# A planned attention kernel: the shared SBUF port in the planner's clock, head groups evened, the opening loads and the last unit's normalisation rearranged

## The chip, the core and the metric

The kernel runs on one core of a Trainium2 chip. Five engines each run their own queue of instructions in order and meet only at semaphores: TensorE (PE, with its weight loads shown as PEld), ScalarE (ACT), VectorE (DVE), GpSimd (POOL) and SyncE (SP), which here only starts DMA transfers. ACT starts a few transfers too. The metric is device time in microseconds of the whole program. The kernel before took 675.31 us (median of 7 runs, 674.93 to 677.05).

## The reference, cut to what matters

Two attention blocks over 2048 tokens of width 512, with 32 heads of 16 columns each; their outputs stand side by side.

```python
qkv = (x @ wqkv)  # -> q, k, v per head, 32 heads of 16
# A: linear attention
phi = lambda t: jnp.where(t > 0, t + 1, jnp.exp(t)) + 1e-6
o = (phi(q) @ (phi(k).T @ v)) / (phi(q) @ phi(k).sum(0) + 1e-6)
# B: full softmax attention
p = softmax(q @ k.T * 16 ** -0.5)
o = p @ v
# both: o, heads joined, @ wo; A in columns 0:512, B in 512:1024
```

Block B is nearly all of the work: 32 heads of 2048 x 2048 exponentials.

## The kernel before, in words

**Units and blocks.** B is cut into 32 units, taken in order. A unit is a group of eight heads (`Gp`, four of them), a chunk of 512 queries (`c`, four), and the even or odd heads of the group (`e_`, two): four heads, one for each of the four 32-row bands of TensorE ("head group" g). Each of these four heads has 16 blocks of 128 keys x 512 queries, so a unit has 64 blocks and the kernel 2048.

**What a block goes through.** A score matmul on PE (L785, 32 rows; blocks of different g run side by side in different bands) puts 128x512 scores into a PSUM bank. Then one of two engines makes the exponential. ACT takes two or three banks in one instruction (L1000), each block leaves one tile, and one matmul with the values (L1129, "PV", into a 32-column band of the bank `PVb`; again four g side by side) uses it. Or DVE takes one bank, sometimes two (L886): it makes an exponential of low precision by integer arithmetic on the bits, POOL makes two shifted copies (L1075, `int64_add`, mostly two blocks an instruction), and the three copies are weighted and averaged by three PV matmuls with weights folded into copies of V (L632). So a block on DVE spares ACT its share, and costs PE three PV matmuls in place of one, DVE one instruction and POOL two halves.

**Closing a unit.** When all PV matmuls of a unit are done, `unit_done` (L1149) has DVE transpose `PVb` (L1153), take the reciprocal of the sums (L1160), multiply (L1161) and, after every second unit, transpose back into the output operand `ON` (L1167). The next unit's PV matmuls can start after L1153. The last unit's four output tiles (`last_tiles`, L1190) have three quarters of their matmuls done ahead; the fourth (L1181) waits for L1167, then DVE and ACT copy two tiles each (L526), and each tile is stored by a DMA (L1201), from SP's queue for DVE's tiles and from ACT's for ACT's.

**The planner.** The order of all instructions is fixed when the program is built, by a simulated clock: `T` holds the time at which each engine comes free, `cands` the ready stages with a planned length, `opts` the next choice of each engine, and the earliest goes next. `fill_act_cand` gives blocks to ACT (two or three from `choose`), with blocks for DVE (`d_pick`) put into the same score phase up to four in all; `fill_d_cand` gives DVE more; `pv_cand` forms PV batches of one or two, sometimes three, rounds of up to four g; `job_cand` fits in the projections and block A; `fill_in` puts dummy matmuls (L1351) into gaps of PE. `d_pick` gives DVE a block only if DVE's planned backlog is small. `choose` takes the head groups by "not used in this phase", then most blocks left. `TABLE` holds eleven settings of these rules for each 20 us of planned time (waits, backlogs, batch sizes, reserves). The planner knows nothing of DVE and POOL holding each other up. The chip runs the queues in the planned order, whenever the semaphores let it.

**The opening.** ACT's queue loads tokens 256 to 511 of B_x (L384, into `ON[:, 2:4]`) and the K weights of group 0; SP's queue loads tokens 0 to 255 with a transposing DMA (L393), the Q weights of group 0, tokens 512 to 1023 (transposing), the V weights, and the rest. PE runs 30 warm-up matmuls (L1209), transposes the two plain tiles (L1220; copies by DVE and ACT, L526), and projects the first K and Q tiles (L1231), which DVE and ACT copy out (L1239, L1241, L1243). The planner's clock starts behind this with written-in times.

Of the kernel before, what the change touches and what calls it, by code (L numbers as in the profile page):

```python
# [17 lines left out]
class _Op:  # L18
    __slots__ = ("idx", "lane", "fn", "pos", "waits", "sig", "count", "vc",
                 "name", "queue")  # L20

# [219 lines left out]
def bass_concat_heads__linear_attn_block__softmax_full_mha__prompt_kernel(nc, A_x, A_wqkv, A_wo, B_x, B_wqkv, B_wo, out):  # L241
# [34 lines left out]
        (3, 0.1, 1.0, 0, 16, 8, 2, 0.8, 0, 4.0, 4),  # L276
        (3, 0, 1.0, 0.6, 16, 8, 2, 0.8, 0, 4.0, 4),
        (1, 0.05, 2.0, 1.0, 16, 11, 2, 0.8, 0.5, 3.0, 6),
        (1, 0.05, 2.0, 0.6, 16, 11, 2, 2, 0.5, 3.0, 8),
        (1, 0.05, 2.0, 1.0, 8, 12.5, 2, 2, 0.5, 3.0, 8),  # L280
        (2, 0.3, 0.6, 0, 5, 8, 3, 0.8, -0.5, 4.0, 4),
        (2, 0.3, 0.6, 0, 5, 13.5, 2, 0.8, -0.5, 4.0, 4),
        (3, 0.3, 0.6, 0, 16, 13.5, 2, 0.8, -0.5, 4.0, 4),
        (3, 0.3, 0.6, 0, 16, 13.5, 2, 0.8, 0.8, 4.0, 8),
        (3, 0.05, 0.6, 1.0, 6, 9, 2, 0.8, 0.5, 4.0, 4),
        (3, 0.05, 1.0, 0.6, 16, 13.5, 3, 0.8, 0.2, 3.0, 4),
        (2, 0.2, 0.3, 0.6, 12, 8, 2, 0.8, 0.5, 2.0, 4),
        (1, 0.2, 1.5, 0.6, 3, 11, 2, 0.8, 0.5, 4.0, 6),
        (1, 0.2, 1.5, 0.3, 3, 11, 2, 0.8, 0.5, 4.0, 6),
        (2, 0.2, 1.5, 0.3, 3, 12.5, 2, 0.8, 0.2, 2.0, 8),  # L290
        (2, 0.2, 1.5, 0, 3, 9, 2, 0.8, 0.2, 2.0, 8),
        (3, 0.05, 0.6, 0.6, 12, 8, 2, 0.8, 0.2, 2.0, 6),
        (3, 0.2, 0.6, 0.6, 12, 10, 2, 2, -0.5, 3.0, 8),
        (3, 0.1, 1.0, 0.3, 8, 10, 2, 2, 0.2, 4.0, 8),
        (1, 0.2, 1.5, 0.3, 8, 9, 2, 0.8, 0, 4.0, 8),
        (2, 0.3, 1.0, 1.0, 16, 9, 2, 2, 0.2, 3.0, 6),
        (2, 0, 0.3, 1.0, 16, 9, 2, 2, 0.2, 3.0, 6),
        (2, 0.2, 1.5, 0, 12, 13.5, 3, 0.8, 0.2, 4.0, 8),
        (3, 0.3, 2.0, 0, 12, 12.5, 2, 0.8, 0, 2.0, 8),
        (1, 0, 2.0, 1.0, 5, 13.5, 2, 0.8, 0, 3.0, 8),  # L300
        (1, 0.3, 2.0, 0, 12, 13.5, 2, 0.8, 0.5, 3.0, 8),
        (2, 0.05, 2.0, 0, 12, 11, 2, 0.8, 0.5, 3.0, 8),
        (2, 0.05, 2.0, 0, 12, 11, 2, 0.8, 0.2, 3.0, 8),
        (3, 0.3, 1.0, 1.0, 3, 10, 2, 2, -0.5, 4.0, 6),
        (2, 0, 2.0, 1.0, 16, 11, 2, 0.8, 0, 4.0, 8),
        (1, 0.2, 2.0, 0.6, 16, 10, 2, 2, 0.8, 2.0, 4),
        (1, 0, 1.5, 0.3, 16, 8, 2, 0.8, -0.5, 3.0, 8),
        (1, 0, 2.0, 1.0, 5, 12.5, 2, 0.8, 0.8, 4.0, 6),
# [10 lines left out]
    with es:  # L319
# [75 lines left out]
        load(ON[:, 2:4, :], B_x[0].rearrange("(t p) c -> p t c", p=128)[:, 2:4, :], on_keys(2) + on_keys(3), queue="act")  # L395
        load_t(xTb, "xTb", B_x, 0, 2)
        load(Wb[:, :, 512:640], wbv[:, :, 512:640], [("Wb", 1, 0)], queue="act")
        load(Wb[:, :, 0:128], wbv[:, :, 0:128], [("Wb", 0, 0)])
# [220 lines left out]
        def v4_job(t4, Gp, **kw):  # L619
# [11 lines left out]
            for k in (1, 2):  # L631
                st.append(("dve", 0.2, f_op("dve", lambda e, k=k: e.tensor_scalar(  # L632
                    VV[:, r, k, 4 * t4:4 * t4 + 4, :], VV[:, r, 0, 4 * t4:4 * t4 + 4, :], WGT[k], None, op0=ALU.mult),
                    [("VV", t, r) for t in ts] + [("VV1", r)], [("VW", k, t, r) for t in ts])))
# [6 lines left out]
        def phi_stages(c0, n, out_ap, okeys):  # L641
# [4 lines left out]
                ("dve", 0.08 + n * 0.00026, f_op("dve", lambda e: e.tensor_scalar(EA[:, q, 0:n], EA[:, q, 0:n], 1.0, 1e-6, op0=ALU.min, op1=ALU.add),  # L646
# [112 lines left out]
        def choose(u, n, used=()):  # L759

            got, t0 = [], 0.0
            order = sorted(range(4), key=lambda g: (g in used, -len(rem[u][g]), g))
# [25 lines left out]
        def qk_reads(bl):  # L788
            res = []
            for u, j, g in bl:  # L790
                Gp, c, e_ = unit(u)
                res += [("QT", Gp % 2, c), ("KMj", e_, j, g) if Gp % 2 == 0 and j < 4 else ("KM", Gp % 2, e_, j // 4, g)]
                if Gp == c == 0:
                    res += [("QT0", i) for i in range(2)]
# [34 lines left out]
        def d_pick(at, used, keep=()):  # L829
# [12 lines left out]
            ch = choose(u, 1, used)  # L842
# [86 lines left out]
        def fill_act_cand():  # L929
# [24 lines left out]
            def run(st, en):  # L954
                more = bfree[ob] is not None and bfree[ob] <= st and pt_room(3, st + 0.5) is not None
                if more:
                    ids = [x for x in DSET if bfree[x] is not None and bfree[x] <= st]
                    if d_backlog(st) < (DLOW, DLOW2, -1)[len(ids) - 1] and d_pick(st + 0.05, ()) is not None:
                        more = False
                def grow(n):  # L960
                    bl, t0 = choose(u, min(n, left[u]))
                    if len(bl) < n and u + 1 < NU:
                        ch2 = choose(u + 1, n - len(bl), [g for _, _, g in bl])
# [3 lines left out]
                def ok(n):  # L967
                    c_ = choose(u, min(n, left[u]))
# [117 lines left out]
        def pv_cand():  # L1086
# [36 lines left out]
            def run(st, en):  # L1123
# [15 lines left out]
                if todo[u] == 0:  # L1139
                    pvu[0] += 1  # L1140
                    pvopen[0] = None
                    push("dve", en + LPX, -1, 0.64, lambda st_, en_: unit_done(u, en_))
# [6 lines left out]
        def unit_done(u, t_):  # L1149

            xb = (u // 2) % 2
            Gp, c, e_ = unit(u)
            sch.add("dve", lambda e: e.transpose(OT[:, 0, :], PVb[:, 0:512]), reads=[("PV", g) for g in range(4)], writes=[("OT", 0)])  # L1153
            pvopen[0] = t_ + LDP
            if c == NC - 1 and e_ == 1:
# [5 lines left out]
                  ("dve", 0.35, f_op("dve", lambda e: e.tensor_tensor(xn[:, :, 16 * e_:16 * e_ + 16], o[:, :, 0:16],  # L1161
# [8 lines left out]
            if Gp == NGP - 1 and e_ == 1:  # L1170
                if u == NU - 1:
                    last_tiles(t_)
                else:
                    for tl in range(4):
                        urgent2.append(omm_job("b", 4 * c + tl, tl, [("on", Gp, c)], [(1, ("st", c, tl))]))
# [16 lines left out]
        def last_tiles(t_):  # L1192

            last_pre(range(3, 4) if pred[0] else range(4), t_ + 0.01, 0)
            for tl in range(4):
                lane = ("dve", "act")[tl % 2]
                def last(bk, tl=tl):
                    sch.add("pe", lambda e: lt_mm(e, tl, 3), reads=["WOb"] + on_keys(15), writes=[LTB[tl][3]], accum=("lt", tl))
# [309 lines left out]
```

## Time and profile before

| | |
|---|---|
| median of 7 runs | 675.31 us |
| the profiled execution | 675.93 us, its span 674.2 us |
| TensorE clock granted | 0.999 |
| ACT busy | 658.1 us, of it 644 exponentials of L1000 |
| PE busy | 654.9 us |
| DVE busy | 583.6 us, of it 622 instructions of L886 |
| POOL busy | 401.3 us |
| first exponential starts / last ends | 8.44 / 663.57 us |

In a line of groups stand: source line, engine, operation, output<-input, shapes, count, then busy time, mean length in ns of one instruction, and idle time before them. A recorded length of ACT or DVE overlaps the next instruction's, so the pace is the distance of successive ends or starts, not the mean length. In a line of the timeline stand: start, length, engine, line, operation, and how many instructions are merged. Ends of matmuls are modelled.

### The profile page before, as it was taken

How to read it: one execution, taken by the hardware profiler on the slowest of the kernel's cores; microseconds unless marked ns; L12 is line 12 of the kernel's file. 1: busy time of each engine (PE TensorE's matmuls, PEld its weight loads, DVE VectorE, ACT ScalarE, POOL GpSimd, SP SyncE). 2: the span in 40 equal slices, each digit the busy share in tenths (PEclk: the TensorE clock that was granted, in tenths of full speed). 3: DMA queues.
4: the chain of work that ended last, by engine and by line, in shares of the span. 5: the costliest groups of instructions: out<-in, count | busy, mean ns of one | idle time of the engine just before them, and what ended most of it. 6: DMA issues, size and time to landing. Idle time of an engine off the chain costs nothing.

```text
span 674.2 us, 16306 instructions
## 1 busy us (share of the span) xinstructions
PE 654.9 (97%) x6661; PEld 210.9 (31%) x6661; DVE 583.6 (87%) x984; ACT 658.1 (98%) x682; POOL 401.3 (60%) x681
## 2 busy tenths in 40 slices
PE   8999999999999999999999999999999999999996
PEld 4322233433433333323322332233322222222222
DVE  6998898778788989888999899887899997999893
ACT  6999999999999999999999999999999999999994
POOL 5587675335455567554566567545566674778671
PEclk9999999999999999999999999999999999999999
DMA  9920000000000000000010000000100001000001
GB/s 177 242 83 1 1 2 1 11 13 9 5 1 1 2 1 1 10 10 9 18 33 17 10 25 17 18 10 24 26 23 18 9 18 48 24 18 17 18 24 36
DMA packets 36576, 17.36 MB, mean 26 GB/s; under 512 B 27536, under 2 KB 35984, under 8 KB 36496
## 3 DMA queue, kind: packets, MB, share of 16 engines
q1 hardware_dynamic: 35408, 15.61, 10.0%
q8 instruction: 54, 0.88, 0.6%
q10 hardware_dynamic: 1088, 0.66, 0.3%
q14 instruction: 26, 0.21, 0.1%
HBM read 4.46 MB, written 4.19 MB: 13 GB/s over the span
## 4 chain that ended last, share of the span: by engine, by line
ACT 67%; PE 25%; DVE 5%; issue 1%; DMA 1%; SPq 0%; ACTq 0%; DVEq 0%
ACT MEM L1000 65%; PE pPV L1129 10%; PE pS L785 9%; DVE MEM L886 3%; ACT EA L645 2%; PE pS L654 1%; PE pS L548 1%; DMA MEM<-in_B_wqkv_dram 1%; PE pS L733 1%; DVE EA L646 1%; PE pS L680 0%; DVE OT L1153 0%; PE pS L1181 0%; DVE OT L1161 0%; PE pPV L1351 0%
## 5 line engine op out<-in xcount | busy, mean ns | idle before, releaser
L1000 ACT ACTIVATE MEM<-pS 128x1024 f16<-128x1024 f32 (+1 forms) x644 | 646.6, 1242 | 1.7 <-PE pS L785 1.4
L1075 POOL INT64_ADD MEM<-MEM x654 | 393.6, 615 | 258.0 <-DVE MEM L886 229.5
L886 DVE TENSOR_SCALAR MEM<-pS 128x512 int16<-128x512 f32 (+1 forms) x622 | 416.0, 706 | 53.1 <-PE pS L785 49.5
L1129 PE MATMUL pPV<-MEM,VV 128*17 128x512 f16 x3348 | 279.7, 382 | 0.3 <-DVE OT L1153 0.2
L785 PE MATMUL pS<-QT,KM 32*128 32x512 bf16 x2048 | 264.0, 384 | 8.6 <-ACT MEM L1000 5.5
L785 PEld LDWEIGHTS pS<-QT,KM 32*128 32x128 bf16 x2048 | 68.9, 91 | 244.4 <-ACT MEM L1000 202.8
L1129 PEld LDWEIGHTS pPV<-MEM,VV 128*17 128x17 bf16 x3348 | 59.9, 88 | 116.6 <-issue 93.0
L654 PE MATMUL pS<-Wa,xTa 128*128 128x256 bf16 x256 | 38.9, 275 | 0.1
L548 PE MATMUL pS<-MEM 128*128 128x512 bf16 x120 | 36.0, 384 | 0.6 <-DVE KNa L648 0.3
L1153 DVE STREAM_TRANSPOSE OT<-pPV 128x512 f32<-128x512 f32 x32 | 22.7, 709 | 6.7 <-PE pPV L1129 6.5
L654 PEld LDWEIGHTS pS<-Wa,xTa 128*128 128x128 bf16 x256 | 20.0, 97 | 17.9 <-issue 8.8
L645 ACT ACTIVATE EA<-pS 128x512 bf16<-128x512 f32 x32 | 23.2, 724 | 0.0
L526 DVE CAST KNa<-pS 128x512 bf16<-128x512 f32 x30 | 20.4, 681 | 1.1 <-PE pS L1181 0.7
L680 PE MATMUL pS<-xTa,Wa 128*128 128x512 bf16 x64 | 19.5, 384 | 0.6 <-DVE MEM L886 0.4
L733 PE MATMUL pS<-WOa,KNa 128*128 128x512 bf16 x64 | 20.0, 385 | 0.0
L623 PE MATMUL pS<-MEM 128*128 128x128 bf16 x256 | 19.3, 220 | 0.0
L1161 DVE TENSOR_TENSOR OT<-OT,ZR 128x256 bf16<-128x256 f32 x32 | 18.6, 581 | 0.6
L646 DVE TENSOR_SCALAR EA<-EA 128x512 bf16<-128x512 bf16 x32 | 12.6, 393 | 6.2 <-ACT EA L645 5.7
L623 PEld LDWEIGHTS pS<-MEM 128*128 128x128 bf16 x256 | 14.4, 98 | 7.4 <-issue 4.1
L733 PE MATMUL pS<-WOb,MEM 128*128 128x512 bf16 x48 | 14.9, 385 | 0.0
L1351 PE MATMUL pPV<-ZW 128*17 128x256 bf16 x75 | 14.5, 274 | 0.0
L548 PEld LDWEIGHTS pS<-MEM 128*128 128x128 bf16 x120 | 8.2, 97 | 18.6 <-issue 10.1
(80 smaller groups left out, 213.0 us busy)
## 6 DMA issues: line engine op xcount, KB each, us to landing
out_dram<-KNa SPq DMA_DIRECT2D x30, 128.0 KB, 1.7
Wa<-in_A_wqkv_dram SPq DMA_DIRECT2D x1, 1536.0 KB, 7.5
KM<-KR SPq DMA_DIRECT2D x96, 16.0 KB, 1.8
MEM<-in_B_wqkv_dram SPq DMA_DIRECT2D x2, 384.0 KB, 5.7
MEM<-in_B_wqkv_dram SPq DMA_DIRECT2D x1, 512.0 KB, 5.0
WOb<-in_B_wo_dram SPq DMA_DIRECT2D x1, 512.0 KB, 8.4
WOa<-in_A_wo_dram SPq DMA_DIRECT2D x1, 512.0 KB, 9.2
MEM<-in_B_x_dram ACTq DMA_DIRECT2D x1, 256.0 KB, 2.9
```

What stands on the lines that cost most here:

```text
L526: return lambda e, bk: (e.tensor_copy(out_fn(), in_fn(bk)) if lane == "dve" else e.activation(out_fn(), in_fn(bk), ACTF.Copy))
L548: return e.matmul(f32v(bk), lhsT=Wb[:, cc, kind * 512 + Gp * 128:kind * 512 + Gp * 128 + 128], rhs=xTb[:, cc, sc * 512:(sc + 1) * 512], st ...
L623: return e.matmul(f32v(bk)[:, tl * 128:(tl + 1) * 128], lhsT=xTb[:, cc, t * 128:(t + 1) * 128], rhs=Wb[:, cc, 1024 + Gp * 128:1024 + Gp * ...
L645: ("act", 0.06 + n * 0.000833, f_ev("act", lambda e, bk: e.activation(EA[:, q, 0:n], f32v(bk)[:, c0:c0 + n], ACTF.Exp), [], [("EA", q)])),
L654: return e.matmul(f32v(bk)[:, 256 * tt:256 * tt + 256], lhsT=xTa[:, cc, (t2 + tt) * 128:(t2 + tt + 1) * 128], rhs=Wa[:, cc, 512 * kind + 2 ...
L733: return e.matmul(f32v(bk), lhsT=src, rhs=WO[:, hb, :], start=(hb == 0), stop=(hb == 3))
L785: return e.matmul(dst, lhsT=KM[32 * g:32 * g + 32, Gp % 2, e_, j * 128:(j + 1) * 128], rhs=QT[32 * g:32 * g + 32, Gp % 2, c * 512:(c + 1) ...
L886: sch.add("dve", lambda e: e.tensor_scalar(PTi[:, i * 512:(i + n) * 512], PS[:, b0 * 512:(b0 + n) * 512], ESC, EB, op0=ALU.mult, op1=ALU.add),
L1000: sch.add("act", lambda e: e.activation(PT[:, p0 * 512:p0 * 512 + w], PS[:, use[0] * 512:use[0] * 512 + w], ACTF.Exp, scale=SC), reads=[(" ...
L1075: sch.add("pool", lambda e: e.int64_add(PTl[:, pos * 128:pos * 128 + w], PTl[:, p0 * 128:p0 * 128 + w], v_), reads=[("PT", p0 + i) for i i ...
L1129: sch.add("pe", lambda e, g=g, j=j, hl=hl, pi=pi, k=k, first=first, last_=last_: e.matmul(PVb[32 * g:32 * g + 17, 0:512], lhsT=VV[:, Gp % ...
L1153: sch.add("dve", lambda e: e.transpose(OT[:, 0, :], PVb[:, 0:512]), reads=[("PV", g) for g in range(4)], writes=[("OT", 0)])
```

## The change

Five things.

1. **Port.** A class `_Port(float)` marks the planned lengths of three DVE steps: the V copies of L632, the clamp of block A's exponential (L646) and the multiply of L1161. Such a step starts, in the plan, when both DVE and POOL are free, and keeps POOL for its length. Two planned lengths are retouched.
2. **Head groups.** For DVE's blocks `choose` now prefers the head group with the fewest PV matmuls in this unit so far, done and due; and the score phase of ACT looks up DVE's next pick first and leaves its group out of ACT's choice.
3. **Opening.** All of tokens 0 to 511 come by two plain loads from SP's queue; K and Q weights of group 0 both come from ACT's queue; PE transposes four tiles; the second half of Q is made tile by tile; K for the odd heads is copied out after all K for the even heads. The written-in times are new.
4. **Ending.** The last unit's four DVE steps are each done in two column halves, in turn; the first two output tiles need only the first half. Tile 0 and 2 are copied by ACT, 1 and 3 by DVE; tiles 0 and 1 are stored from SP's queue, 2 and 3 from ACT's.
5. **Settings.** All 33 rows of `TABLE` are other numbers, and `fill_in` leaves room for a change of matmul kind.

```diff
+class _Port(float):
+    pass
...
-                st.append(("dve", 0.2, f_op("dve", lambda e, k=k: e.tensor_scalar(
+                st.append(("dve", _Port(0.21), f_op("dve", lambda e, k=k: e.tensor_scalar(
...
+                    if isinstance(c_[3], _Port):
+                        st = max(st, T["pool"])
...
+            if isinstance(dur, _Port):
+                lo = max(st, T["pool"])
+                T["pool"] = lo + dur
+                dur = lo - st + dur
...
-        def choose(u, n, used=()):
+        def choose(u, n, used=(), dv=False):
-            order = sorted(range(4), key=lambda g: (g in used, -len(rem[u][g]), g))
+            order = sorted(range(4), key=lambda g: (g in used, (pv_rem[u][g] + pv_iss[u][g]) if dv else 0, -len(rem[u][g]), g))
...
-            ch = choose(u, 1, used)
+            ch = choose(u, 1, used, True)
...
+                pk0 = d_pick(st + 0.05, ())
+                gd = [pk0[0][2]] if pk0 is not None else []
                 def grow(n):
-                    bl, t0 = choose(u, min(n, left[u]))
+                    bl, t0 = choose(u, min(n, left[u]), gd)
...
-        load(ON[:, 2:4, :], B_x[0].rearrange("(t p) c -> p t c", p=128)[:, 2:4, :], on_keys(2) + on_keys(3), queue="act")
-        load_t(xTb, "xTb", B_x, 0, 2)
+        for t in (0, 2):
+            load(ON[:, t:t + 2, :], B_x[0].rearrange("(t p) c -> p t c", p=128)[:, t:t + 2, :], on_keys(t) + on_keys(t + 1))
         load(Wb[:, :, 512:640], wbv[:, :, 512:640], [("Wb", 1, 0)], queue="act")
-        load(Wb[:, :, 0:128], wbv[:, :, 0:128], [("Wb", 0, 0)])
+        load(Wb[:, :, 0:128], wbv[:, :, 0:128], [("Wb", 0, 0)], queue="act")
...
-        tok[("Q", 0, 0)] = 8.0
+        tok[("Q", 0, 0)] = 7.5
...
+        def last_unit(u, t_):
+            for h in range(2):
+                sch.add("dve", lambda e, h=h: e.transpose(OT[:, 0, hs(h)], PVb[:, hs(h)]), reads=[("PV", g) for g in range(4)],
...
+            for h in range(2):
+                sch.add("dve", lambda e, h=h: e.reciprocal(ZR[:, 0, 8 * h:8 * h + 8], v(OT[:, 0, :], h)[:, :, 16]), reads=[("OTh", h)],
...
+            for h in range(2):
+                sch.add("dve", lambda e, h=h: e.tensor_tensor(v(XN[:, xb, :], h)[:, :, 16:32], v(OT[:, 0, :], h)[:, :, 0:16],
...
+            for h in range(2):
+                sch.add("dve", lambda e, h=h: e.transpose(ON[:, k, hs(h)], XN[:, xb, hs(h)]), reads=[("XNh", h), ("XN", xb, 0), ("XN", xb, 1)],
...
-                lane = ("dve", "act")[tl % 2]
+                lane = ("act", "dve")[tl % 2]
...
-                                          reads=kst(tl), queue="act" if lane == "act" else "sp", force_signal=True))
+                                          reads=kst(tl), queue="act" if tl >= 2 else "sp", force_signal=True))
...
-            n = min(int((st - T["pe"] - FM) / 0.107), 24)
+            n = min(int((st - T["pe"] - FM - (0 if mode[0] == "p" else SW)) / 0.107), 24)
```

## The prediction

> **What bounds the kernel now.** First the page's busy table, then the groups by shape, to see which engine has no idle time and what its time is made of.
>
> ```profile
> PE 654.9 (97%) x6661; PEld 210.9 (31%) x6661; DVE 583.6 (87%) x984; ACT 658.1 (98%) x682; POOL 401.3 (60%) x681
> L1000 ACT ACTIVATE MEM<-pS 128x1024 f16<-128x1024 f32 x534 | 520.2, 1172 | 0.7 <-PE pS L785 0.4
> L886 DVE TENSOR_SCALAR MEM<-pS 128x512 int16<-128x512 f32 x594 | 384.0, 682 | 49.6 <-PE pS L785 46.2 <-POOL MEM L1075 0.5
> L1129 PE MATMUL pPV<-MEM,VV 128*17 128x512 f16 x3348 | 279.7, 382 | 0.3 <-DVE OT L1153 0.2
> L1000 ACT ACTIVATE MEM<-pS 128x1536 f16<-128x1536 f32 x110 | 171.1, 1580 | 1.0 <-PE pS L785 1.0
> ```
>
> ACT makes 534 x 2 + 110 x 3 = 1398 of the 2048 blocks, DVE the other 650 (594 single, 28 pairs). In the timeline's single rows the ends of successive exponentials lie 0.917 us apart for 128x1024 and 1.344 for 128x1536, and 0.489 for L645. So ACT's own work is 534 x 0.917 + 110 x 1.344 + 32 x 0.489 = 653.1 us, between 8.44 (first start) and 663.57 (last end): 655.1 us. At most 2.0 us in the middle is waiting. The time is therefore opening (8.4) + ACT's work + ending (10.6), and the middle changes only as blocks change hands: one block moved to DVE takes 0.917 / 2 = 0.4585 us off ACT.
>
> What keeps DVE from taking more? The windows and the timeline of PE say.
>
> ```profile
> 20.00:100.00 80.00, 78.41 (x829) 23.60 (x828) 74.64 (x120) 79.82 (x85) 56.88 (x95) 1.00 0.25 57
> 100.00:500.00 400.00, 394.54 (x4036) 132.78 (x4032) 343.85 (x588) 399.66 (x412) 218.56 (x364) 1.00 0.05 12
> 500.00:660.00 160.00, 156.89 (x1575) 41.66 (x1575) 148.31 (x244) 159.83 (x169) 113.89 (x190) 1.00 0.07 20
> ```
>
> Columns: window, length, busy us of PE, PEld, DVE, ACT, POOL. ACT is full in all three; DVE has room from 100 to 500 (86%), less outside (93%). L886 stood idle 49.6 us, 46.2 of it for scores from PE: DVE waits for PE.
>
> ```profile
> 107.52 0.40 PE L1129 MATMUL pPV<-MEM,VV 128*17 128x512 f16 x4
> 107.84 0.41 PE L785 MATMUL pS<-QT,KM 32*128 32x512 bf16 x3
> 108.19 0.39 PE L1129 MATMUL pPV<-MEM,VV 128*17 128x512 f16 x3
> 108.51 0.61 PE L654 MATMUL pS<-Wa,xTa 128*128 128x256 bf16 x4
> 656.84 0.39 PE L785 MATMUL pS<-QT,KM 32*128 32x512 bf16 x4
> 657.17 0.61 PE L1129 MATMUL pPV<-MEM,VV 128*17 128x512 f16 x8
> 657.76 0.39 PE L785 MATMUL pS<-QT,KM 32*128 32x512 bf16 x3
> ```
>
> A score phase takes 0.33 (656.84 to 657.17) and eight PV matmuls 0.59: together 0.92, just what ACT needs for two blocks. PE goes from one to the next without a hole. And three PV matmuls take as long as four (0.32 from 107.52 to 107.84 and from 108.19 to 108.51): an empty place in a round costs as much as a full one.
>
> **Head groups (part 2).** Counted over the timeline, the 3348 PV matmuls come in 444 runs: 223 of eight, 47 of four, but 40 of seven, 24 of three, 23 of two, 19 of six. Rounded up to full rounds these are 892 rounds, against 3348 / 4 = 837: 55 rounds, or 220 places, are empty, a lower bound as merged runs hide some. A round costs (0.59 - 0.32) = 0.27 at most; the median lengths to the next instruction, 0.56 for eight and 0.33 for four, give 0.23; I take 0.22: 55 x 0.22 = 12.1 us of PE. Choosing DVE's blocks by fewest PV matmuls evens the four bands (a DVE block brings three PV matmuls, an ACT block one), so batches end together. Bounds: nothing, or all 12.1. I take half, 6.05, since batches are also short for want of finished exponentials, which evenness doesn't mend. A block moved costs PE two more places, 0.11 us, and shortens the time by 0.4585; so 6.05 us of PE carries 6.05 / (0.4585 + 0.11) = 10.6 blocks. DVE needs 0.61 for each (start to start of L886 in a row), 6.5 of its 90 idle us; POOL is at 60%.
>
> [...] The rows decide for me: the phases follow each other without a hole, at 0.92 for ACT's 0.917.
>
> **Port (part 1) and settings (part 5).** The marked steps are stretched when POOL runs (least / median / longest ns):
>
> ```profile
> L646 DVE TENSOR_SCALAR EA<-EA x32: 252/324/743, 66.7 to 526.6; 128x512 bf16<-128x512 bf16 x32
> L1161 DVE TENSOR_TENSOR OT<-OT,ZR x32: 409/518/847, 37.8 to 665.1; 128x256 bf16<-128x256 f32 x32
> ```
>
> Those that met no POOL instruction took 0.287 (L646, L632) and 0.425 (L1161); the means are 0.393, 0.398 and 0.581. Stretch: 32 x (0.106 + 0.111 + 0.156) = 11.9 us of DVE that the plan of before didn't hold. ACT's 2.0 us of waiting is all that a truer plan can win directly; I count 0 of it. The other way, a planner that sees DVE busier gives it fewer blocks. Outside 100 to 500, where DVE is at 93%, stand 27 of the 96 steps, 27 x 0.124 = 3.4 us, or 3.4 / 0.61 = 5.5 blocks; the whole 11.9 us would be 19.5. I take 2.6: blocks lost where DVE is full, and not all, as a postponed block mostly finds a place later. The new settings no row can price: the bound is a few per cent of the 650 blocks either way, and I take 0. The smaller `fill_in` takes dummies out of PE's gaps (89 L1351 matmuls, spaced about 0.107 us, 9.5 us in all), which I count as nothing: a gap gained there is a gap anyway. Together: 10.6 - 2.6 = 8 blocks more, 658; ACT's work falls by 8 x 0.4585 = **3.7 us**.
>
> **Opening (part 3).** The first exponential waits for Q, Q for its weights:
>
> ```profile
> 2.23 0.56 SPq L384 DMA_DIRECT2D MEM<-in_B_wqkv_dram  x1
> 5.63 0.38 PE L1231 MATMUL pS<-MEM 128*128 128x128 bf16 x4 [0.92 <-DMA MEM<-in_B_x_dram]
> 6.36 1.71 PE L1231 MATMUL pS<-MEM 128*128 128x256 bf16 x16 [0.34 <-DMA MEM<-in_B_wqkv_dram]
> 8.44 1.45 ACT L1000 ACTIVATE MEM<-pS 128x1536 f16<-128x1536 f32 x1 [1.05 <-PE pS L785]
> ```
>
> On SP that load stands behind a transposing DMA whose issue takes 1.36; it lands 4.1 after its start, at 6.32. On ACT it stands second: K weights issue at 0.80, Q's at 1.28, and land by the same 4.1 at 4.9 and 5.4. The ACT table load starts at 1.79 as before. SP now issues two plain loads (0.44 each, by ACT's row for the same size) and then the transposing DMA of tokens 512 to 1023 at about 1.7 instead of 2.85, everything behind it 1.1 earlier; its packets now run beside both weight loads, so these may gain little. PE transposes four tiles rather than two (eight matmuls more, about 0.6) behind the warm-up that ends at 4.1; DVE and ACT make one copy more each (0.42 and 0.60). These chains end near 5.4 (DVE) and 5.9 (ACT); the second is what is late next, ahead of Q's last tile. From there Q's evacuations and the score phase: Q's first half at 5.9 instead of 6.36, the last score 7.5 instead of 8.0. I take **-0.5**; bounds 0 (the weights land no earlier) and -0.9 (the whole advance of Q's weights).
>
> **Ending (part 4).**
>
> ```profile
> 664.07 0.72 DVE L1153 STREAM_TRANSPOSE OT<-pPV 128x512 f32<-128x512 f32 x1 [4.75 <-PE pPV L1129]
> 667.61 0.37 ACTq L1201 DMA_DIRECT2D out_dram<-KNa  x1
> 668.08 0.60 ACT L526 ACTIVATE KNa<-pS 128x512 bf16<-128x512 f32 x1 [0.51 <-PE pS L1181]
> 668.71 1.43 ACTq L1201 DMA_DIRECT2D out_dram<-KNa  x1
> ```
>
> The four DVE steps take 2.21 (664.07 to 666.28), each waiting for the one before. In halves there are eight, and every second one is independent, so that a result is finished while the next runs. Nearest rows: L1239 starts 0.258 apart for 128 columns and 0.392 for 256, that is 0.124 fixed and 0.00105 a column. By these the halves are 2 x (0.39 + 0.13 + 0.26 + 0.39) = 2.34 plus 0.09 to finish, 2.43; by half of L886's 0.61 they are about 2.0. I take 2.2: second half no earlier, first half 0.4 earlier. What changes more: ACT no longer issues a store (0.37) between its two copies, but issues two after them, the second behind DVE's second copy. That copy ends near 667.9 to 668.1 and the last issue starts near 668.2 instead of 668.71. I take **-0.5**, bounds +0.2 and -0.8; the 1.43 of the last issue I leave as it is.
>
> [...]
>
> **Sum.** -3.7 - 0.5 - 0.5 = -4.7: the profiled execution would go from 675.93 to 671.2. That execution is 0.62 above the median of the seven runs, so against 675.31 the forecast is 670.6.
>
> **Rivals.** (a) *Evening pays fully*, and the settings use it: 12.1 us of PE, 21 blocks, no block lost: -9.6 - 1.0, 664.7. For it: DVE has 90 us free. Against: 93% in the two outer stretches. (b) *The middle doesn't move*: PV batches are short for want of exponentials, or the gain is spent on blocks refused by the port rule; only opening and ending count: 674.3. (c) *Slower: the port rule starves DVE.* `d_pick` compares DVE's planned backlog with a limit, and the plan now holds up to 11.9 us more of it; POOL's planned time also moves back, so the tiles come free later. Each block handed back costs 0.4585: all 19.5 give +8.9 - 1.0, 683.2; ten give 678.9. It decides the sign when DVE makes fewer than 648 blocks, and shows as slower (over 0.2%) under about 645. For it: DVE is full at both ends of the kernel. Against: ACT waited only 2.0 us with the too hopeful plan, and DVE waits for PE, not PE for DVE.
>
> **Chances.** Forecast, 668 to 673.5: 0.58. (a) and beyond: 0.14. (b), about 674.3: 0.12. (c): 0.16. A measurement of this kernel can tell 0.2% (1.35 us) from no change, so faster 0.72, within 0.12, slower 0.16. The range leaves out the far half of (a) and most of (c): 665.0 to 677.5.
>
> **What would show it.** Blocks: L1000's two counts and L886's give DVE's share; 658 expected. PV runs of seven, six, three and two become rare, 444 runs fall. First exponential near 7.9. Last store issue 0.5 nearer to the last exponential. L646 and L1161 nearer to 0.287 and 0.425 if the plan keeps them clear of POOL. The forecast is wrong if DVE's count doesn't rise, or if ACT, full now, begins to wait for scores.

## The result, and the profile after

The changed kernel takes **674.01 us** (median of 16 runs, 672.23 to 675.20), against 675.67 for the kernel before in the same comparison: ratio 0.9970, 95% interval 0.9963 to 0.9978, that is 0.3% faster. The forecast was 670.6. The profiled execution took 674.12 us (span 672.3), 1.8 less than the one before; the forecast had 4.7 less.

First the groups by shape of the changed kernel, with the busy table's line ahead of them.

```profile
PE 651.6 (97%) x6691; PEld 210.6 (31%) x6691; DVE 579.0 (86%) x983; ACT 656.5 (98%) x684; POOL 402.0 (60%) x684
...
L1006 ACT ACTIVATE MEM<-pS 128x1024 f16<-128x1024 f32 x536 | 523.6, 1195 | 1.1 <-PE pS L789 0.9
...
L890 DVE TENSOR_SCALAR MEM<-pS 128x512 int16<-128x512 f32 x578 | 376.3, 684 | 53.4 <-PE pS L789 48.9 <-POOL MEM L1081 0.7
L1135 PE MATMUL pPV<-MEM,VV 128*17 128x512 f16 x3356 | 273.0, 383 | 1.2 <-DVE OT L1162 0.8 <-ACT MEM L1006 0.2
...
L1006 ACT ACTIVATE MEM<-pS 128x1536 f16<-128x1536 f32 x107 | 170.6, 1611 | 0.8 <-PE pS L789 0.8
...
L890 DVE TENSOR_SCALAR MEM<-pS 128x1024 int16<-128x1024 f32 x38 | 46.4, 1221 | 4.2 <-PE pS L789 3.8
```

Read the counts, not the means. ACT makes 536 x 2 + 107 x 3 + 1 = 1394 blocks, DVE 578 + 38 x 2 = 654. Before it was 1398 and 650. Four blocks changed hands; the forecast had eight. L890 still idles for scores from PE (48.9 us, before 46.2). ACT is as full as before:

```profile
20.00:100.00 80.00, 78.47 (x842) 23.75 (x843) 75.89 (x124) 79.95 (x86) 58.38 (x98) 1.00 0.22 53
100.00:500.00 400.00, 393.08 (x4058) 131.13 (x4053) 340.55 (x583) 399.74 (x412) 220.61 (x370) 1.00 0.05 12
500.00:660.00 160.00, 156.43 (x1601) 42.64 (x1602) 146.56 (x238) 158.93 (x169) 112.46 (x187) 0.99 0.07 21
```

These are the three windows of before (after the length: busy us of PE, PEld, DVE, ACT, POOL, then granted clock). Only the last has an ACT gap above 0.3 us (158.93 of 160) and a clock below 1.00; that gap returns below.

The span divides as the prediction divided it. "Waiting" is what the distances of successive ends of ACT's exponentials exceed their pace by (0.917, 1.344 and 0.489 us), summed where it is more than 0.01 us. The second profile of the same changed kernel is the run c_after; e_tail is the best version by one line, told below.

| us | before | changed | c_after | e_tail |
|---|---|---|---|---|
| first exponential starts | 8.44 | 8.49 | 8.46 | 8.08 |
| from there to the last one's end | 655.13 | 653.38 | 652.04 | 651.99 |
| of it ACT waiting | 2.12 | 2.05 | 0.71 | 0.65 |
| last exponential's end to span's end | 10.64 | 10.44 | 10.48 | 9.22 |

So the gain lies in the middle: 1.8 us by four blocks (4 x 0.4585), and in c_after 1.4 us more by less waiting, as the clock stays full there. In the first profile of the changed kernel a stretch at half clock takes this 1.4 us back. The opening gave nothing, the ending 0.2.

### The profile page after: what moved, and what is told of

The parts are those of the page before. It is cut to its first block, busy times and chain, and to the rows that moved or that the text cites. A ratio compares the mean times of both kernels' runs of the same rounds, so it can differ in the third digit from the quotient of the medians.

```text
span 672.3 us, 16395 instructions
## 1 busy us (share of the span) xinstructions
PE 651.6 (97%) x6691; PEld 210.6 (31%) x6691; DVE 579.0 (86%) x983; ACT 656.5 (98%) x684; POOL 402.0 (60%) x684
## 4 chain that ended last, share of the span: by engine, by line
ACT 80%; PE 15%; DVE 1%; issue 1%; DMA 1%; POOL 0%; SPq 0%; ACTq 0%; DVEq 0%
ACT MEM L1006 78%; PE pPV L1135 6%; PE pS L789 6%; ACT EA L649 2%; PE pS L627 1%; PE pS L552 1%; DMA MEM<-in_B_x_dram 1%; PE pS L684 0%; DVE MEM L890 0%; PE pS L1208 0%; POOL MEM L1081 0%; PE pS L1259 0%; PE pS L658 0%; DVE EA L650 0%; DVE KNa L530 0%
## 5 line engine op out<-in xcount | busy, mean ns | idle before, releaser
L890 DVE TENSOR_SCALAR MEM<-pS 128x512 int16<-128x512 f32 (+1 forms) x616 | 419.6, 717 | 57.6 <-PE pS L789 52.7
L1135 PE MATMUL pPV<-MEM,VV 128*17 128x512 f16 x3356 | 273.0, 383 | 1.2 <-DVE OT L1162 0.8
L1135 PEld LDWEIGHTS pPV<-MEM,VV 128*17 128x17 bf16 x3356 | 57.1, 88 | 113.7 <-issue 91.3
L1170 DVE TENSOR_TENSOR OT<-OT,ZR 128x256 bf16<-128x256 f32 x31 | 14.3, 460 | 0.2
L650 DVE TENSOR_SCALAR EA<-EA 128x512 bf16<-128x512 bf16 x32 | 11.2, 349 | 3.7 <-ACT EA L649 3.3
```

Of the source, the lines that this page charges most:

```text
L890: sch.add("dve", lambda e: e.tensor_scalar(PTi[:, i * 512:(i + n) * 512], PS[:, b0 * 512:(b0 + n) * 512], ESC, EB, op0=ALU.mult, op1=ALU.add),
L1135: sch.add("pe", lambda e, g=g, j=j, hl=hl, pi=pi, k=k, first=first, last_=last_: e.matmul(PVb[32 * g:32 * g + 17, 0:512], lhsT=VV[:, Gp % ...
```

## Experiments

**The theories.** When the result was seen, three explanations of the missing gain stood against each other. *Settings*: the evened head groups do free PE time, but the eleven settings per 20 us don't turn it into blocks for DVE. *No PE time freed*, or PE wasn't the limit: evening is worth little, and four blocks is what it can give. *Lost again outside the middle*: the filling rule and the clock, the opening, the order of the queues at the end. In each diff below, the first lines are those of the kernel that is named; a ratio is always against the kernel before on the same chip.

| kernel | median us | kernel before there | ratio, 95% interval |
|---|---|---|---|
| c_after, the changed kernel again | 672.77 | 675.48 | 0.9949 [0.9932, 0.9966] |
| e_tail | 671.1 | 675.1 | 0.9940 [0.9925, 0.9954] |
| e_tail_again | 672.3 | 675.31 | 0.9952 [0.9937, 0.9967] |
| e_tailfill | 671.62 | 675.31 | 0.9935 [0.9918, 0.9951] |
| e_fill | 673.0 | 675.1 | 0.9960 [0.9945, 0.9975] |
| e_oldopen | 673.21 | 675.1 | 0.9967 [0.9954, 0.9979] |
| e_open2 | 672.73 | 675.26 | 0.9951 [0.9932, 0.9970] |
| e_guard | 673.62 | 675.26 | 0.9975 [0.9965, 0.9985] |
| e_slackB10 | 680.05 | 675.48 | 1.0060 [1.0041, 1.0079] |
| e_slackA10 | 673.59 | 675.1 | 0.9974 [0.9964, 0.9985] |
| e_slackA3 | 683.29 | 675.31 | 1.0115 [1.0096, 1.0134] |
| e_newset | 696.65 | 675.48 | 1.0302 [1.0275, 1.0329] |
| e_oldset | 693.07 | 675.48 | 1.0249 [1.0222, 1.0276] |
| e_evened | 678.52 | 675.26 | 1.0041 [1.0024, 1.0058] |
| e_uneven | 693.44 | 675.26 | 1.0262 [1.0241, 1.0284] |

### Is PE the limit, and is there room on it now? e_slackB10, e_slackA10, e_slackA3

A dose of dummy matmuls (0.107 us each) is put in after every tenth (A3: every third) choice of a score phase: B10 is the kernel before with 64 of them (6.9 us of PE), A10 the changed kernel with 63 (6.8 us), A3 with 219 (23.4 us).

```diff
-        def fill_in(st):
+        def fill_in(st, force=0):
...
+            n = max(n, 0) + force
...
-                fill_in(st)
+                qn[0] += md == "q"
+                fill_in(st, 1 if md == "q" and qn[0] % 10 == 0 else 0)
```

> The kernel before with one dummy matmul more ahead of every tenth score phase, 64 more, 6.9 us of PE, else the same order. Theory 'PE bounds DVE's share and so the time': the kernel before has no such room, so it rises by 3 to 6.9 us, to 678 or more, while the changed kernel took the same dose at no measurable cost. Theory 'PE has room in both; DVE's share comes from the settings': under 1 us, 675 to 676.

> The changed kernel with one dummy matmul (128x17 by 256 columns, about 0.11 us) more ahead of every tenth score phase: 63 more, 6.8 us of PE, else the same order. Theory 'PE is what bounds DVE's share and so the time': the changed kernel has only the 34 rounds, 7.5 us, that evening the head groups freed, so it takes most of this and rises by 0 to 2 us; the same dose in the kernel before should cost up to 6.8. Theory 'PE has room to spare in both, and the settings decide DVE's share': the same small cost in both kernels, under 1 us.

> The changed kernel with one dummy matmul more ahead of every third score phase, 219 more, 23.4 us of PE. Theory 'PE's freed time lies unused, about as much as evening freed': 7 to 10 us of the dose vanish, the rest shows, 684 to 690. Rival 'PE has much more room than that, it was never near a limit': under 4 us, below 678. Rival 'the small dose only happened to fall into gaps': the whole 23 us, 696.

Before, the dose cost 680.05 - 675.48 = 4.6 us of its 6.9. After, the same dose left the ratio at 0.9974 [0.9964, 0.9985], where the changed kernel has 0.9970 [0.9963, 0.9978] and 0.9949 [0.9932, 0.9966]: between nothing and 1.7 us. The waits of ACT, first B10, then A10 (us in total, times, longest):

```profile
ACT MEM L1000 <- PE pS L785: 4.2, 6, 1.5
```

```profile
ACT MEM L1006 <- PE pS L789: 0.5, 1, 0.5
```

By the pace, ACT waits 6.8 us in B10 (before: 2.1) and 1.0 in A10 (c_after: 0.7). So PE did limit the kernel before, and after the change PE has time that nothing uses. How much, the large dose tells: 23.4 us cost 683.29 - 674.01 = 9.3, or 10.5 against c_after, with ACT waiting 11.9; 13 to 14 us vanish, more than the 7 to 10 that were expected. "PE wasn't the limit" and "no PE time freed" both fall. What keeps DVE from using this time, the doses don't say.

The weight loads take 31% of the span in both kernels (PEld 210.9 and 210.6 us), PE's matmuls 97% (654.9 and 651.6 us). So neither share tells which kernel has room on PE; the doses do (4.6 us of 6.9 before, 0 to 1.7 of 6.8 after).

### What are the settings worth? e_newset, e_oldset

The tables are exchanged: e_newset is the kernel before with the new `TABLE` (its first two of 33 rows below), e_oldset the changed kernel with the old one.

```diff
-        (3, 0.1, 1.0, 0, 16, 8, 2, 0.8, 0, 4.0, 4),
-        (3, 0, 1.0, 0.6, 16, 8, 2, 0.8, 0, 4.0, 4),
...
+        (3, 0, 1.5, 0, 16, 11, 2, 2, -0.5, 2.0, 8),
+        (1, 0, 1.5, 1.0, 16, 9, 2, 2, -0.5, 2.0, 8),
...
```

> The kernel before with nothing changed but the 33 rows of settings, taken from the changed kernel. DVE gets 612 blocks instead of 650. Theory 'the settings fit only the rules they were searched for, and time follows the blocks': 38 x 0.4585 = 17.4 us more work for ACT, so 693, plus what ACT waits in an order that nobody searched. Theory 'the new settings are better ones': no slower than before.

> The changed kernel with the 33 rows of settings of the kernel before: port rule, evened head groups, opening and ending are all there. DVE gets 609 blocks instead of 654, in 881 rounds of PV matmuls planned where the changed kernel plans 899. Theory 'time follows the blocks, and the settings set them': 45 x 0.4585 = 20.6 us more than the changed kernel, about 694.5, whatever PE saves. Theory 'evening by itself frees PE and so time': faster than the kernel before, under 675.

The ACT groups, e_newset first:

```profile
L1000 ACT ACTIVATE MEM<-pS 128x1024 f16<-128x1024 f32 x505 | 496.2, 1163 | 3.8 <-PE pS L785 3.5
L1000 ACT ACTIVATE MEM<-pS 128x1536 f16<-128x1536 f32 x142 | 217.5, 1598 | 1.2 <-PE pS L785 1.1
```

```profile
L1006 ACT ACTIVATE MEM<-pS 128x1024 f16<-128x1024 f32 x500 | 498.1, 1193 | 0.7 <-PE pS L789 0.7
L1006 ACT ACTIVATE MEM<-pS 128x1536 f16<-128x1536 f32 x146 | 230.2, 1619 | 0.6 <-PE pS L789 0.5
...
L1006 ACT ACTIVATE MEM<-pS 128x512 f16<-128x512 f32 x1 | 0.8, 835 | 0.0
```

ACT makes 1436 blocks in e_newset and 1439 in e_oldset. So either way DVE is left with far fewer: 612 and 609, and the time rises by 21.2 and 17.6 us against the kernel before. (e_newset doesn't compute the right result, its relative error is 0.13, and why isn't known; its time stands for an order of instructions only. e_oldset carries the point without it.) At 0.4585 a block, 650 - 612 = 38 blocks are 17.4 us, and 650 - 609 = 41 are 18.8; e_newset adds 5.8 us of waiting, 3.7 more than before; e_oldset has 1.6. Neither table carries over to the other rules: the new rules with the old table lose 41 blocks, the new table with the old rules 38, and the two together win 4. The prediction's bound for the settings, "a few per cent of the 650 blocks either way", was the right size (6%), and it set the term to 0.

### Evening with equally fitted settings: e_evened, e_uneven

So the rules have to be compared with settings of equal fit. For both kernels the same random search was made: from the old settings, 800 changes of single rows, each kept if the planned end comes no later. e_evened has all the rules of the change; e_uneven is the same without the evening of head groups.

```diff
-            order = sorted(range(4), key=lambda g: (g in used, (pv_rem[u][g] + pv_iss[u][g]) if dv else 0, -len(rem[u][g]), g))
+            order = sorted(range(4), key=lambda g: (g in used, -len(rem[u][g]), g))
...
-                gd = [pk0[0][2]] if pk0 is not None else []
+                gd = []
```

> The changed kernel with settings found by a small search of its own: from the settings of the kernel before, 800 random changes of single rows, each kept if the planned end comes no later. DVE gets 647 blocks (609 at the start of the search). Theory 'evening pays, once settings are sought under it': its partner without evening, sought in the same way with the same 800 draws, gets 617, so this one is faster by 30 x 0.4585 = 13.8 us; itself 7 blocks short of the changed kernel, 3.2 us slower than it, near 677. Theory 'evening is worth nothing, the search alone makes the blocks': the two take the same time within 2 us.

> The partner: the changed kernel without the evening of head groups (both edits of it undone), port rule, opening and ending as in the changed kernel, settings sought by the same 800 draws from the same start. DVE gets 617 blocks. First theory: 37 blocks short of the changed kernel, 17 us, near 691, 13.8 slower than its partner. Second theory: like its partner.

They differ by 693.44 - 678.52 = 14.9 us. The ACT groups, e_evened first:

```profile
L1006 ACT ACTIVATE MEM<-pS 128x1024 f16<-128x1024 f32 x558 | 543.0, 1200 | 3.0 <-PE pS L789 2.9
...
L1006 ACT ACTIVATE MEM<-pS 128x1536 f16<-128x1536 f32 x95 | 152.5, 1623 | 0.8 <-PE pS L789 0.8
```

```profile
L1006 ACT ACTIVATE MEM<-pS 128x1024 f16<-128x1024 f32 x499 | 497.7, 1191 | 2.4 <-PE pS L789 2.3
...
L1006 ACT ACTIVATE MEM<-pS 128x1536 f16<-128x1536 f32 x144 | 225.9, 1618 | 1.4 <-PE pS L789 0.9
```

Their blocks for DVE are 647 and 617: 30 blocks, 13.8 us, and the rest within the waiting of ACT (4.4 and 5.1 us; either profile holds two stretches of half clock). In this pair evening is worth far more than the whole change brings. But it is one pair of random searches, and how much of the 30 blocks is the luck of the draw no run shows. Two more searches of each kind, counted in the plan and shown by no run, gave 626 and 630 with evening against 611 and 621 without: the same sign, and a smaller size.

After 800 draws DVE has 617 blocks without evening, where the kernel before, also without it, has 650. So that kernel's settings seem fitted much closer than 800 draws fit. Whether the changed kernel's table is fitted as closely to its rules isn't shown, and how far a longer search under the new rules would go stays open. With it stays open whether the unused PE time can become blocks at all, or whether something else holds DVE back.

### The ending: e_tail, e_tail_again

```diff
-                                          reads=kst(tl), queue="act" if tl >= 2 else "sp", force_signal=True))
+                                          reads=kst(tl), queue="act" if tl == 2 else "sp", force_signal=True))
```

Tile 3, which DVE copies, is stored from SP's queue instead of ACT's.

> The changed kernel with one store moved: output tile 3 (copied by DVE) is stored from SP's queue, not from ACT's. Theory 'the ending lost its gain to the queue': in the changed kernel ACT's store of tile 3 stands ahead of ACT's copy of tile 2 and made that copy wait 1.4 us, so without it ACT's second copy starts near 665.3 of that profile instead of 666.6, the last store issue comes about 1 us earlier, and the time falls from 674.0 to about 673.0 (ratio to the kernel before about 0.9960). Rival 'the tail after the last exponential is set by something else, such as the time a store takes to land': less than 0.3 us.

> The changed kernel with tile 3 stored from SP's queue, as the yardstick on this chip: ratio 0.9940 by the earlier run, 0.9925 to 0.9965 if the dip comes more often than in the earlier five executions.

The timeline of ACT at the end of the changed kernel, and then of e_tail (start, length):

```profile
664.60 0.60 ACT L530 ACTIVATE KNa<-pS 128x512 bf16<-128x512 f32 x1 [2.74 <-PE pS L1208]
666.14 0.37 ACTq L1228 DMA_DIRECT2D out_dram<-KNa  x1
666.61 0.60 ACT L530 ACTIVATE KNa<-pS 128x512 bf16<-128x512 f32 x1 [1.42 <-DVE KNa L530]
667.24 1.09 ACTq L1228 DMA_DIRECT2D out_dram<-KNa  x1
```

```profile
662.80 0.60 ACT L530 ACTIVATE KNa<-pS 128x512 bf16<-128x512 f32 x1 [2.74 <-PE pS L1208]
...
663.88 0.60 ACT L530 ACTIVATE KNa<-pS 128x512 bf16<-128x512 f32 x1 [0.48 <-PE pS L1208]
664.51 0.37 ACTq L1228 DMA_DIRECT2D out_dram<-KNa  x1
```

In the changed kernel ACT's second copy "waits for DVE", though it reads nothing of DVE's. Between the two copies stands the store at 666.14: it is tile 3's, it needs DVE's copy, and everything behind it on ACT waits along: ACT idles 1.42 us between the two copies. With that store on SP it idles 0.48, and the stretch from the last exponential to the end falls from 10.44 to 9.22. In the five profiles with this order it is 9.2 to 9.6; in the nine of the changed ending without it, 10.3 to 10.7, but for one of 9.7 (e_slackA3) and one of 11.1 (e_fill). About 1 us, then. By the ratios e_tail and e_tail_again (0.9940 and 0.9952) lie below the result's 0.9970, but e_tail_again is level with c_after's 0.9949, and these intervals overlap. So the profiles carry this reading and the medians don't settle it.

### The opening: e_oldopen, e_open2

e_oldopen is the changed kernel with the old loads, transposes and copies. e_open2 is e_tail with tokens 256 to 511 first on ACT's queue, and Q's weights behind tokens 0 to 255 on SP's:

```diff
-            load(ON[:, t:t + 2, :], ..., on_keys(t) + on_keys(t + 1))
+            load(ON[:, t:t + 2, :], ..., on_keys(t) + on_keys(t + 1), queue=("sp", "act")[t // 2])
...
-        load(Wb[:, :, 0:128], wbv[:, :, 0:128], [("Wb", 0, 0)], queue="act")
+        load(Wb[:, :, 0:128], wbv[:, :, 0:128], [("Wb", 0, 0)])
```

> The changed kernel with the loads and first instructions of the kernel before, and the planner's written-in times of the changed one, so that the order behind the opening is the same. Theory 'the new opening is worth nothing' (first exponential at 8.49 after, 8.44 before): 674.0, within 0.3 us of the changed kernel, first exponential near 8.44. Rival 'the profiled execution had a late clock (full from 6.05 us, against 3.88 before) and hid a gain': the changed kernel's opening is worth up to the forecast 0.5 us, so this one is slower than it by about 0.5, 674.5.

> The changed kernel with tile 3 stored from SP's queue (as in the run before that did this alone, ratio 0.9940) and with two loads exchanged: tokens 256 to 511 come first on ACT's queue, the Q weights second on SP's. Theory 'the second token load, issued at 1.34 and landing at 5.3 to 5.7, now ends the opening': it lands at about 4.6 with the first, the score phase starts near 7.3 instead of 7.65 to 8.1, and the ratio falls by 0.0005 to 0.0008, to about 0.9933. Rival 'the weights are then the last to land, or all share the same transfer rate': the opening stays, ratio 0.9940.

With the old opening the first exponential starts at 8.41 in e_oldopen and 8.44 in the kernel before, with the new one at 8.49 in the changed kernel, and the ratios agree (0.9967 and 0.9970; c_after, on the same chip as e_oldopen, has 0.9949, with an interval that overlaps). Two stretches of the chain of waits, from the changed kernel and from e_tail (start, length), and a line of PE's timeline from c_after:

```profile
1.34 4.11 DMA MEM<-in_B_x_dram
...
5.49 0.87 PE pS L1249 x8
6.36 1.78 PE pS L1259 x24
```

```profile
1.34 3.94 DMA MEM<-in_B_x_dram
...
5.33 0.62 PE pS L1249 x8
5.95 1.77 PE pS L1259 x24
```

```profile
5.71 0.62 PE L1249 MATMUL pS<-identb,MEM 128*128 128x128 bf16 x8 [0.43 <-DMA MEM<-in_B_x_dram]
```

The second plain load of tokens is issued at 1.34 and lands at 5.24 to 5.66 in the twelve profiles that have it on SP's queue. Behind it stand eight transposes and 24 matmuls, 0.62 + 1.77 under a clock full early (e_tail), up to 1.03 and 2.06 under one full late (e_fill). When the clock became full differed between two executions of the same kernel: 6.05 in the changed kernel's profile, 4.31 in c_after.

Both moments count. In eight profiles the clock was full by 5.5 us, and the first exponential starts 2.8 to 2.9 us behind the landing: at 8.04 where that came at 5.25, at 8.46 in c_after, where it came at 5.66, on average at 8.19. So the early clock alone didn't bring the 8.05 expected of c_after. In four in which the clock was full at 6.05 to 6.92, the first exponential comes 3.0 to 3.5 us behind the landing, at 8.47 to 8.88. The old opening was seen in four profiles, all with a clock full by 4.59 (8.37 to 8.55, on average 8.44). So under an early clock the new one is some 0.25 us better on average; what the old one does under a late clock stays open. In e_open2 both token loads had landed by 4.93, but the clock was full only at 6.95 and the first exponential came at 8.91. Whether that order would pay under an early clock isn't settled.

### The clock's dip: c_after, e_fill, e_tailfill, e_guard

e_fill takes the old filling rule back (133 dummies in the plan for 99), e_tailfill does so in e_tail, and e_guard adds up to four dummies a score phase in e_tail, in 10 us of the plan around the dip.

```diff
-            n = min(int((st - T["pe"] - FM - (0 if mode[0] == "p" else SW)) / 0.107), 24)
+            n = min(int((st - T["pe"] - FM) / 0.107), 24)
```

```diff
-                fill_in(st)
+                fill_in(st, 4 if md == "q" and 523 < T["pe"] < 533 else 0)
```

> The changed kernel itself once more, as the yardstick for the kernels beside it: 673.4 to 674.0 by both theories. Theory 'the clock's phase sets the opening, and a dip of the clock near 535 us comes in some executions and not in others': executions with a granted clock of 0.997 or more lie 1 to 1.5 us under those with 0.994, and the first exponential of the profile starts near 8.05 where the clock is full by 4.8 us and near 8.5 to 8.9 where it is full only after 6. Rival 'both are fixed by the order of the instructions': 8.49 and a dip again.

> The changed kernel with the rule of before for dummy matmuls in PE's gaps: 133 of them instead of 99, the order of all else is the same, instruction by instruction. Theory 'thinner filling let the clock gate close': the changed kernel's profile shows half the clock from 535.1 to 538.5 us and ACT waiting 1.4 us there; with more dummies the granted clock should be 0.997 or more in most runs and the time about 1.2 us lower, 672.8. Rival 'the dip comes from the order of the work itself' (a stretch of small matmuls around 531 to 535): the dip stays and the time is 674.0, or a little higher for the 34 more dummies.

> The same with the rule of before for dummies in PE's gaps (133 instead of 99). Theory 'thinner filling let the clock gate close': no execution under a clock of 0.996, median at least 0.7 us below the yardstick beside it. Rival 'the dip comes of the order of the work': the same share of executions with a low clock and the same time within 0.5 us.

> The changed kernel with tile 3 stored from SP's queue and with up to four dummy matmuls ahead of each score phase from 523 to 533 us of planned time, 31 more in all, where PE was busy for 2.47 of 3.5 us ahead of the dip of the clock. Theory 'the dip comes of PE being too little busy in that stretch and of the phase of the clock gate': no execution dips any more, all lie within 0.7 us of the best of the kernel with the moved store alone, ratio 0.9930 to 0.9940. Rival 'the dip is something else, or PE's time counts there': as before or worse, up to 1 us.

Two neighbouring windows of the changed kernel, of c_after and of e_tailfill (the same columns, the granted clock third from the end):

```profile
531.50:535.00 3.50, 2.47 (x28) 1.01 (x27) 3.43 (x7) 3.50 (x5) 2.95 (x5) 1.00 0.00 0
535.00:538.50 3.50, 3.47 (x31) 0.89 (x35) 2.67 (x5) 2.73 (x3) 1.87 (x4) 0.52 0.00 0
```

```profile
531.50:535.00 3.50, 2.50 (x29) 1.04 (x27) 3.42 (x8) 3.50 (x5) 2.92 (x5) 1.00 0.00 0
535.00:538.50 3.50, 3.45 (x50) 1.25 (x54) 3.39 (x7) 3.50 (x4) 1.87 (x4) 1.00 0.02 5
```

```profile
531.50:535.00 3.50, 2.55 (x30) 0.95 (x31) 3.34 (x7) 3.50 (x5) 3.12 (x6) 0.91 0.00 0
535.00:538.50 3.50, 3.50 (x39) 0.83 (x33) 2.69 (x5) 2.69 (x3) 1.22 (x2) 0.60 0.02 5
```

In the first window PE pauses in all three (2.5 of 3.5 us busy: a unit ends there). In the next the clock is half in the first and the third, for 3.41 us, and ACT works 2.7 of 3.5; in c_after, the same program, nothing happens. The dip costs ACT 1.3 to 1.4 us, which is nearly all the waiting that the changed kernel's profile has (2.05 against 0.71). Of the 18 timed and profiled executions of the changed kernel, 15 have a mean clock of 0.996 or less and take 673.4 to 675.2; the three at 0.997 take 672.2 to 673.0. c_after's six have 0.995 to 0.997 and take 672.1 to 673.8. So the median of 674.01 probably holds such a loss in most of its executions, and c_after's 672.77 in fewer. It isn't shown, as the mean clock alone doesn't tell a dip: two of c_after's six have 0.995 and take 672.8 and 672.9, no longer than its profiled one with 0.997 and no dip (672.8).

The filling rule is not its cause: e_tailfill fills by the old rule and dips. Nor does the rule cost anything that can be told: e_fill's interval overlaps those of the changed kernel and c_after. Guarding against it costs more than it: e_guard's profile has no dip (three of its twelve executions, at 0.995, may have one), but its dummies make ACT wait 2.2 us in the guarded stretch, and it is slower than e_tail. Of all these kernels e_tailfill has the lowest ratio, 0.9935, which e_tail's interval doesn't separate from 0.9940.

The stretch at half clock in the changed kernel's profile is 3.413 us long, and in all 17 profiles every stretch between two changes of the clock is a whole number of steps of that length (669.01 us in the kernel before is 196 of them; 529.07 and 129.71 in the changed kernel are 155 and 38). Counted in these steps from the moment at which the clock became full, the pause at the unit's end falls into one step in the three profiles that dip there (the changed kernel, e_tailfill, e_open2), with PE busy for 2.36, 2.46 and 2.40 us of it. In c_after it is spread over two, with 3.02 and 2.75. So PE wasn't idle throughout the step ahead of the dip: it was busy for 2.4 of the 3.4 us. Nor does the busy time alone decide: e_fill has 2.50 in that place and no dip, e_slackB10 a step with 2.23 at 14 us and none, and e_uneven dips behind 2.68.

## Why the prediction was wrong, point by point

**What bounds the kernel: right.** ACT stays full, the middle moved by 0.4585 us per block, and PE was the limit of the kernel before, as the phases without a hole had said (the dose: 4.6 us).

**The failing step: blocks out of the freed PE time, with "The new settings no row can price ... and I take 0".** PE's time was freed as the step said. In the plan the PV matmuls go from 933 rounds to 899, 34 x 0.22 = 7.5 us where 6.05 was taken, and in the profile they are busy for 273.0 us instead of 279.7 (L1135 and L1129), though there are eight more. The prediction's own count over the timeline shows less of it, 892 full rounds to 885 and 444 runs to 440: runs of eight go from 223 to 251, of seven from 40 to 25 and of six from 19 to 8, but those of two and three, which were to become rare, stay (47 to 50). But 7.5 us of PE became four blocks rather than 7.5 / 0.57 = 13, and the dose shows the rest lying idle. How many blocks DVE gets goes with the settings, and these are good only for the rules that they were fitted to (17.6 to 21.2 us lost by exchanging them). So the sum failed in its form: rules and settings don't add as separate terms, -41 and -38 blocks alone, +4 together. Freed PE time was priced as if blocks followed by themselves, and the settings at 0. This is 4 blocks against 10.6 - 2.6 = 8 forecast, 1.9 us of the miss of 2.9 in the profiled execution. Whether the new table is less well fitted than the old one, so that a longer search would bring the other blocks, is argued from e_evened and e_uneven (14.9 us with equal fit) and not shown.

**Port: not separated; no loss of blocks seen.** The steps meet POOL less: means fall from 0.393 to 0.349 (L646), from 0.398 to 0.311 (L632) and from 0.581 to 0.460 us (L1161).

```profile
L650 DVE TENSOR_SCALAR EA<-EA x32: 251/294/739, 65.4 to 529.3; 128x512 bf16<-128x512 bf16 x32
...
L1170 DVE TENSOR_TENSOR OT<-OT,ZR x31: 414/426/795, 49.4 to 657.6; 128x256 bf16<-128x256 f32 x31
```

The median of L1170 is 426 where L1161 had 518, and of the 96 marked steps 77 overlapped a POOL instruction before, and 54 of 95 do now. DVE's busy time falls by 4.6 us. That a truer plan wins nothing directly isn't shown: in c_after ACT waits 0.7 us where it waited 2.1 before, and with an unfitted table 1.6 us under the new rules (e_oldset, a dip included) but 5.8 under the old ones (e_newset). Which rule does it stays open, as no run has the port rule alone; so does the sign of the 2.6 blocks charged to it.

**Opening: wrong, +0.05 instead of -0.5.** The step let all four transposed tiles be ready "behind the warm-up that ends at 4.1" and took the last copy as what is late next. Left out was that the second plain load has to land too: it stands second on SP's queue and lands at 5.24 to 5.66, with eight transposes and 24 matmuls behind it, at half clock in some executions. (Q's weights land at 5.73 in the changed kernel, not at 5.4, but PE comes to them only at 6.19.) With an early clock about 0.25 of it is there, on average.

**Ending: right in kind, mis-sized; -0.2 instead of -0.5.** The halves did what was said: the four DVE steps take 2.07 instead of 2.21 us.

```profile
662.34 0.78 DVE L1189 STREAM_TRANSPOSE OT<-pPV 128x256 f32<-128x256 f32 x2 [4.26 <-PE pPV L1135]
...
663.65 0.76 DVE L1199 STREAM_TRANSPOSE MEM<-OT 128x256 bf16<-128x256 bf16 x2
```

The row per column (2.43) was too long, half of L886 (2.0) nearer. What failed is "ACT no longer issues a store (0.37) between its two copies, but issues two after them": the order on ACT's queue is copy, store of tile 3, copy, store of tile 2, and the first store waits for DVE. The last issue starts 5.38 us after the last exponential's end (667.24 - 661.86), where before it was 5.14.

**What no step held: the clock's dip**, 1.4 us in the execution that was profiled, and probably part of the median. Without it the same plan takes 3.1 us off the middle (c_after), near the 3.7 forecast, but by four blocks and less waiting rather than by eight blocks.

**The rivals.** "The middle doesn't move" gave 674.3 and lies nearest to the result, but not by its mechanism: the middle moved by 1.8 to 3.1 us, and opening and ending didn't. "Evening pays fully" didn't come; whether the rule could give it with other settings stays open. "The port rule starves DVE" didn't happen.

## What to carry to other kernels

Where a plan's settings were searched for one set of rules, a change of the rules is measured only after an equal search, and its forecast needs a range for the fit, as wide as what exchanging the settings costs. Before turning freed time of an engine into gain, dose that engine with dummy work in both versions: a dose that costs nothing says that the time is free and unused. Here one of 6.9 us cost 4.6 before and one of 6.8 cost 0 to 1.7 after, where the busy share was 97% in both. In a queue that works in order, look for the instruction that waits for another engine and for what is queued behind it: here a store that ACT only issued left ACT idle for 1.4 us ahead of its own copy, against 0.5 without it.

## What the hardware showed unexpectedly

The granted clock became full between 3.9 us after the start (the kernel before) and 6.95 (e_open2), differing by execution of even the same kernel (6.05 in the changed kernel, 4.31 in c_after). Where it came late, the first exponential started 3.0 to 3.5 us behind the landing of the tokens it needs, where it came early, 2.8 to 2.9. A half-clock stretch of 3.41 us came with PE busy for 2.47 of the 3.5 us before it (70%) in one execution of a program, and in the next, c_after, with 2.50 of 3.5, none came; in the three profiles that had it near 535 us it came 529.07 us after the clock had become full, 155 steps of 3.413 us. So in these profiles the dip went with the place of the pause on that grid: within one step in these three, spread over two in c_after. How short a pause within a step is enough isn't settled (dips came behind 2.36 to 2.93 us of busy PE, and a step with 2.23 had none).
